# Capped attention before an eight-expert MoE on one core: the exponential of a pair of steps is issued one pair later, value products trail by seven and six steps, joint sums stand in the step without value products

## The chip, the cores and the metric

The kernel runs on one core of a Trainium2 chip. The metric is the device time of one execution in microseconds. Three runs of the kernel before took 822.85, 823.05 and 824.02 us; the median is 823.05 us. A change of 0.2%, about 1.65 us, is about what a measurement of this kernel can tell from none.

## What is computed

```python
scores = (1 / np.sqrt(64)) * np.matmul(q, k.transpose(0, 1, 3, 2))   # 8 batches, 12 heads, 448 x 448
scores = cap * np.tanh(scores / cap)                                 # cap = 30
attn = np.exp(scores - scores.max(-1, keepdims=True))
attn = attn / (attn.sum(-1, keepdims=True) + 1e-09)
x = np.matmul(attn, v)                      # laid out as 3584 tokens x 768
logits = x @ w_gate + modality_bias[modality_id]
e_idx = np.argmax(logits, axis=1)
gate_w = softmax(logits)[np.arange(N), e_idx]
for e in range(8):                          # each token goes to one expert
    h = np.maximum(x[e_idx == e] @ w1[e], 0.0)          # 768 -> 1024
    out[e_idx == e] = gate_w * (h @ w2[e])              # 1024 -> 768
```

The change lies in the attention alone; the experts follow it and are the same in both kernels.

## The kernel before

The attention is cut into 24 *units* (`ND`), each of four heads of one batch, three units to a batch. A unit has seven *steps* of 64 keys (`STEPS`), so there are 168 steps. Step `n` is step `s` of unit `d`, with `n = 7 d + s`. One loop over `n` in `attention` writes all of it out by hand; `pin` keeps an instruction in that order on its engine. Instructions without `pin` (most of the routing) are placed by the tile framework.

Work of one step:

- `scores(n)` (L489): four fp32 matmuls on quarters of the TensorE array write the 64 keys x 448 queries of four heads into a PSUM tile `sc`, of which there are two. ScalarE reads it with one tanh (L494) and writes one half of a *pair* tile `pt`; steps `2k` and `2k+1` share pair `k`. After the tanh of an odd step one exponential (L497) runs in place over the pair. Five pair tiles rotate.
- `add` (L510): VectorE adds the exponentials of a unit into `tot`, four steps behind the scores (`BEHIND`).
- `weigh(m)` (L522): four matmuls on quarters of the array multiply the exponentials of an earlier step `m` with the values and accumulate into `xT`, one PSUM tile for all units. When step 6 of a unit has been weighed, `keep` (L529) copies `xT` to SBUF on VectorE. The first value product of the next unit has to wait for that copy. How far `weigh` trails is a table: `PLAGS = (5, 5, 5, 4, 4, 4, 4)` by the step of the unit. By it, step 0 of a loop unit has two value products, step 4 has none (the *free step*), the others have one.
- `sums2` (L561, L563): in the free step of every even unit, eight matmuls on column strips make the denominators and the gate products of the last two units from their `tot` and `kept` tiles; `gl` (L567) copies the result out.
- `turn2` (L552): in step 4 of every odd unit, four transposes turn it over; VectorE takes reciprocals (L580) and products `lg` (L603).
- `start_route` and `go_on`: when a batch is complete (six times in the units 5 to 19, all odd: 5, 7, 11, 13, 17, 19), step 5 of that odd unit begins the routing: a chain of small VectorE instructions that each read the one before (`L` L250, L253, then L258 to L277, `before` and `acc` L283, L284), a small exponential on ScalarE, and two small matmuls (`rank`, L290, L292) in the next even unit.
- `tokens` (L613), a VectorE transpose, and loads and stores on SP's queue once per unit.

The last four units (`d >= PAIRED = 20`) have lags of their own (`LAGS`, `LAST`).

Of the kernel before, what the change touches and what calls it, by code (L numbers as in the profile page):

```python
# [43 lines left out]
AF = mybir.ActivationFunctionType  # L44
# [10 lines left out]
STEPS = S // KB  # L55
# [22 lines left out]
ND = NU * B  # L78
PAIRED = ND - 4
LAGS = ((5, 5, 5, 5, 4, 4, 3), (6, 5, 5, 5, 4, 4, 3))  # L80
PLAGS = (5, 5, 5, 4, 4, 4, 4)
LAST = (4, 4, 4, 4, 4, 4, 4)
BEHIND = 4

# [1 line left out]
class Program:  # L86
# [7 lines left out]
    def pin(self, inst):  # L94
        return self.tc.keep_in_program_order(inst)
# [359 lines left out]
    def attention(self, firsts, rp, xp):  # L455
        tc, nc = self.tc, self.nc
        pe, pin, V = nc.tensor, self.pin, nc.vector
        with ExitStack() as st:
# [8 lines left out]
            vas, pts, tots, kept, lgs, pays, gls, lts, raws, xss, routing = {}, {}, {}, {}, {}, {}, {}, {}, {}, {}, []  # L467

            def fetch(d):
                if d < ND:  # L470
                    for g in (2 * d, 2 * d + 1) if d else ():
                        self.load_kq(ring[g % 4], g)
                    vas[d] = ld.tile([128, VW], F32, name="va")
                    self.load(vas[d], self.v[d // NU, d % NU])

            def weights(n):
                if n % 2 == 0:
                    pts[n // 2] = pp.tile([128, 4, S], F32, name="pt")
                return pts[n // 2][:, n % 2 * 2 : n % 2 * 2 + 2]

            def scores(n):

                d, s = divmod(n, STEPS)
                sc = ps_s.tile([128, 2, 512], F32, name="sc")
                for i in range(2):
                    kq = ring[(2 * d + i) % 4]
                    for j in range(2):
                        rows = slice(j * D, (j + 1) * D)
                        pin(pe.matmul(  # L489
                            sc[i * KB : (i + 1) * KB, j, :S], kq[rows, s * KB : (s + 1) * KB], kq[rows, S:QK],  # L490
                            start=True, stop=True,
                        ))
                slow = n // STEPS == SOON + 2 and 2 <= n % STEPS <= 5
                pin(nc.scalar.activation(weights(n), sc[:, :, :S], AF.Tanh, scale=self.isc if slow else self.iscr))  # L494
                if n % 2:
                    pt = pts[n // 2]
                    pin(nc.scalar.activation(pt, pt, AF.Exp, scale=self.cabsr))  # L497

            direct = [n for d, steps in {ND - 1: 2}.items() for n in range(STEPS * d + STEPS - steps, STEPS * d + STEPS)]

# [75 lines left out]
            def turn2(a):  # L576

                lt = flip(gls.pop(a))
                for u in range(2):
                    pin(V.reciprocal(recs(a + u), lt[:, :, 2 * u : 2 * u + 2, GE : GE + 2]))  # L580
                    lts[a + u] = lt[:, :, 2 * u : 2 * u + 2]
# [12 lines left out]
            def logits(d):  # L594

                b, r = divmod(d, NU)
                lt = lts.pop(d)
                rec = pays[b][:, :, RECS:].rearrange("p c (j k) -> p c j k", j=2)
                if r == 0:
                    lgs[b] = xp.tile([CP, C, H, E], F32, name="lg", bufs=2)  # L600
                for i in range(2):
                    h0 = 4 * r + 2 * i
                    pin(V.tensor_tensor(  # L603
                        lgs[b][:, :, h0 : h0 + 2], lt[:, :, i, :GE].rearrange("p c (j e) -> p c j e", j=2),
                        rec[:, :, :, 2 * r + i].unsqueeze(3).to_broadcast([CP, C, 2, E]), op=ALU.mult,
                    ))
# [10 lines left out]
            def store(b, queue=nc.sync):  # L617
                xs = xss.pop(b).rearrange("p m k b -> p m (k b)")
                wide = KC * HB
                for g in range(4):  # L620
                    j, h = divmod(g, 2)
                    o = (2 * h + j) * wide
                    put = queue.dma_start(
                        self.xd[b * S : (b + 1) * S, o : o + wide].rearrange("(m a) f -> a m f", a=HB),
                        xs[g * HB : (g + 1) * HB],
                    )
                    if queue is nc.sync:
                        self.last_sp = pin(put).ins
# [8 lines left out]
            def go_on():  # L637
                for way in routing:
                    next(way, None)
# [13 lines left out]
            END = STEPS * ND  # L653
            due = [[] for _ in range(END + 1)]
            for m in range(END):
                d, s = divmod(m, STEPS)
                due[min(m + (LAST if d == ND - 1 else PLAGS if d < PAIRED else LAGS[d % 2])[s], END)].append(m)
            added, held = 0, range(STEPS * (SOON + 2), STEPS * (SOON + 2) + 5)

            def more(n, count=0):  # L660
                nonlocal added
                while (n not in held or count > 0) and added <= n - BEHIND + (n >= END - STEPS):
                    add(added)
                    added += 1
                    count -= 1
                    if count == 0:
                        break
# [3 lines left out]
            for n in range(END):  # L671
                d, s = divmod(n, STEPS)
                if s == 0:
                    fetch(d + 1)
                    if 1 < d < SOON and d % NU == 1:
                        store(d // NU - 1)
                    if d == 0:
                        self.fetch_bias()
                    if d == 1:
                        self.blank(xp.tile([128, FF], F32, name="spare", bufs=2))  # L680
                    if 0 <= d - 2 < CLEAR:
                        self.empty_map(d - 2)
                scores(n)
                late = False
                if not late:
                    more(n)
                if (d, s) == (1, 3):
                    self.gate_bias()
                if (s == 6 or s == 1) and d != SOON + 2:
                    go_on()  # L690
                if s == 4 and d % 2 and 3 <= d < PAIRED + 3:
                    turn2(d - 3)
                    go_on()
                    logits(d - 3)
                    logits(d - 2)
                if s == 4 and d % 2 == 0 and 2 <= d <= PAIRED:
                    sums2(d - 2)
                if (d, s) == (SOON + 1, 5):
                    sums(SOON)
                if s == 5 and d % 2 and 3 <= d < PAIRED + 2:  # L700
                    for u in (d - 3, d - 2):
                        if u % NU == NU - 1:
                            start_route(u // NU)
                if (d, s) == (SOON + 2, 2):
                    more(n, 2)
                for m in due[n]:
                    weigh(m)
                    if m % STEPS == STEPS - 1:
                        keep(m // STEPS)
                if s == 2 and d % NU == 2:  # L710
                    tokens(d - 2)
                if s == (4 if d == SOON + 1 else 6) and 0 < d < ND - 1 and d % NU != 1:
                    tokens(d - 1)
                    if d == SOON + 1:
                        store(d // NU - 1)
                if d == SOON + 2 and {2: 0, 3: 1, 4: 9}.get(s):
                    more(n, {2: 0, 3: 1, 4: 9}[s])
                if (d, s) == (SOON + 1, 6):
                    turn(SOON)
                    logits(SOON)  # L720
                    start_route(SOON // NU, firm=True)
                    go_on()
                    go_on()
                if (d, s) == (SOON + 2, 1):
                    go_on()
                    meta = self.early_slot(self.cpool, self.ps_r)
                    self.first_e = self.expert(meta, 0)
                    load_w1((0, 1), self.first_e)
                if (d, s) == (SOON + 2, 4):
                    maps = self.rows(meta, 0, early=True)  # L730
                    got = self.gather(maps, known=NT - S)
                    load_w1((2, 3, 4, 5), self.register(nc.gpsimd, meta[0:1, 0:1], E - 1, got.ins), nc.gpsimd)
                if d == SOON + 3 and s >= STEPS - TW:
                    self.norm(maps, s - (STEPS - TW))
# [20 lines left out]
            last = []  # L755
# [577 lines left out]
```

## Time and profile before

| | |
|---|---|
| median of three runs | 823.05 us (822.85 to 824.02) |
| the profiled execution | 822.63 us, of which its span is 821.0 us |
| TensorE's granted clock | 0.998 of full speed over the span |
| busy over the span | PE 803.3 us, VectorE 519.3 us, ScalarE 516.3 us, GpSimd 140.2 us |
| attention | first tanh at 7.57 us, last exponential of the attention ends at 300.5 us |

Times in the rows count from the span's start. In the timeline, equal instructions that follow each other on an engine are one row ("x8"); each fp32 matmul of the program shows as two instructions, so the four matmuls of a step are a row "x8". A busy PE is not a full PE, since the ends of matmuls are modelled; the starts of successive rows tell more.

### The profile page before, as it was taken

What the parts mean: (1) busy time and instruction counts of PE and PEld (TensorE: products, weight loads), DVE (VectorE), ACT (ScalarE), POOL (GpSimd) and SP (SyncE); (2) the same over time, 40 slices, a digit from 0 to 9 for tenths busy, and PEclk for the clock granted to TensorE, in tenths of its full rate; (3) what the DMA queues carried; (4) which work ended last, traced back from release to release, by engine and by line L of the source; (5) the groups of instructions that cost most, each with busy time, mean ns of one, the idle gap of its engine ahead of it and who ended that gap; (6) DMA issues with size and microseconds to landing.
All of it is one profiled execution on the core that took longest, in us unless ns stands there. A gap on an engine that the chain in (4) does not pass through costs nothing. (4 is left out here: it accounts for less than half of the span.)

```text
span 821.0 us, 15448 instructions
## 1 busy us (share of the span) xinstructions
PE 803.3 (98%) x5988; PEld 608.8 (74%) x5988; DVE 519.3 (63%) x865; ACT 516.3 (63%) x655; POOL 140.2 (17%) x163
## 2 busy tenths in 40 slices
PE   7999999999999999999999999999999999999996
PEld 2333333333333348999999999999999999989996
DVE  4778888888788988764445354452544635447662
ACT  6999999999999994453444334444254442556572
POOL 2000220012021230451303113031120310111010
PEclk9999999999999999999999999999999999999999
DMA  5375536255453652977656365563665545557670
GB/s 180 122 224 187 156 118 203 91 182 167 150 160 136 188 200 63 265 250 270 217 172 219 125 213 214 189 209 129 205 232 182 212 146 178 167 201 242 217 231 20
DMA packets 57011, 148.44 MB, mean 181 GB/s; under 512 B 7758, under 2 KB 22366, under 8 KB 56928
## 3 DMA queue, kind: packets, MB, share of 16 engines
q1 hardware_dynamic: 48224, 113.34, 43.1%
q0 software_dynamic: 8560, 34.02, 11.4%
q8 instruction: 49, 0.80, 0.4%
q14 instruction: 34, 0.28, 0.1%
q10 hardware_dynamic: 144, 0.00, 0.0%
HBM read 114.44 MB, written 24.64 MB: 169 GB/s over the span
## 5 line engine op out<-in xcount | busy, mean ns | idle before, releaser
L957 PE MATMUL ph<-x,al 128*128 128x384 f32 (+2 forms) x510 | 160.3, 314 | 0.0
L1010 PE MATMUL py<-bh,hh 128*128 128x384 f32 x464 | 158.8, 342 | 0.4 <-ACT hh L968 0.2
L1010 PE MATMUL py<-bl,hh 128*128 128x384 f32 x464 | 155.8, 336 | 0.0
L1010 PE MATMUL py<-bh,hl 128*128 128x384 f32 x464 | 155.7, 336 | 0.0
L522 PE MATMUL xT<-pt,va 64*64 64x448 f32 x1344 | 151.6, 538 | 0.5 <-DVE xT L529 0.5
L494 ACT ACTIVATE pt<-sc 128x896 f32<-128x896 f32 x164 | 142.8, 905 | 11.3 <-PE sc L489 11.2
L497 ACT ACTIVATE pt<-pt 128x1792 f32<-128x1792 f32 x84 | 142.7, 1698 | 2.7
L510 DVE TENSOR_TENSOR tot<-tot,pt 128x896 f32<-128x896 f32 x118 | 127.8, 1083 | 10.8 <-ACT pt L497 6.4
L953 PE MATMUL ph<-x,ah 128*128 128x384 f32 x366 | 122.6, 335 | 0.0
L954 PE MATMUL ph<-x,ah 128*128 128x384 f32 x366 | 122.4, 335 | 0.0
L896 DVE TENSOR_TENSOR bl<-raw,bh 128x768 fp32r<-128x768 f32 x88 | 81.3, 955 | 50.7 <-ACT bh L895 50.6
L522 PEld LDWEIGHTS xT<-pt,va 64*64 64x64 f32 x1344 | 50.6, 133 | 72.9 <-issue 68.4
L1026 ACT ACTIVATE ot<-py,mt 128x384 f32<-128x384 f32 (+1 forms) x58 | 33.4, 577 | 105.9 <-PE py L1010 68.6
L968 ACT ACTIVATE hh<-ph 128x384 fp32r<-128x384 f32 x64 | 31.3, 492 | 106.1 <-PE ph L957 97.9
L957 PEld LDWEIGHTS ph<-x,al 128*128 128x128 f32 x510 | 96.2, 189 | 0.0
L1010 PEld LDWEIGHTS py<-bh,hh 128*128 128x128 f32 x464 | 87.1, 188 | 1.1 <-ACT hh L968 0.5
L896 DVE TENSOR_TENSOR al<-raw,ah 128x1024 fp32r<-128x1024 f32 x60 | 70.9, 1222 | 26.7 <-ACT ah L895 26.7
L1010 PEld LDWEIGHTS py<-bl,hh 128*128 128x128 f32 x464 | 87.2, 188 | 0.0
L1010 PEld LDWEIGHTS py<-bh,hl 128*128 128x128 f32 x464 | 87.1, 188 | 0.0
L895 ACT CAST bh<-raw 128x768 fp32r<-128x768 f32 x88 | 70.0, 836 | 22.4 <-DMA raw<-in_w_dram 20.9
L489 PE MATMUL sc<-kq 64*64 64x448 f32 x672 | 79.6, 548 | 4.5 <-ACT pt L494 3.2
L923 DVE TENSOR_TENSOR x<-ptr,x 128x384 fp32r<-128x384 f32 (+2 forms) x64 | 31.6, 516 | 76.0 <-ACT x L922 76.0
(183 smaller groups left out, 957.6 us busy)
## 6 DMA issues: line engine op xcount, KB each, us to landing
raw<-in_w_dram SPq DMA_DIRECT2D x88, 384.0 KB, 4.5
raw<-in_w_dram SPq DMA_DIRECT2D x62, 512.0 KB, 4.3
kq<-in_kq_dram SPq DMA_DIRECT2D x24, 448.0 KB, 3.9
va<-in_v_dram SPq DMA_DIRECT2D x24, 448.0 KB, 5.4
kx<-in_kq_dram SPq DMA_DIRECT2D x24, 448.0 KB, 4.1
xd<-xs SPq DMA_DIRECT2D x32, 336.0 KB, 6.3
xr<-xg POOLq DMA_DIRECT2D x24, 384.0 KB, 3.1
mapd<-spare SPq DMA_DIRECT2D x4, 480.0 KB, 6.7
```

The lines of the kernel that those rows point to most:

```text
L489: pin(pe.matmul(sc[i * KB : (i + 1) * KB, j, :S], kq[rows, s * KB : (s + 1) * KB], kq[rows, S:QK], start=True, stop=True,))
L494: pin(nc.scalar.activation(weights(n), sc[:, :, :S], AF.Tanh, scale=self.isc if slow else self.iscr))
L497: pin(nc.scalar.activation(pt, pt, AF.Exp, scale=self.cabsr))
L510: pin(V.tensor_tensor(tots[d], pt_of(n - 1) if s == 1 else tots[d], pt_of(n), op=ALU.add))
L522: pin(pe.matmul(self.xT[j * D : (j + 1) * D, i, :S], vas[d][rows, o : o + D], pt[rows, j], start=s == 0, stop=s == STEPS - 1,))
L895: keep((cast.tensor_copy if cast else self.nc.scalar.copy)(hi, raw))
L896: keep((minus or self.nc.vector).tensor_tensor(lo, raw, hi, op=ALU.subtract))
L953: keep(nc.tensor.matmul(ph[:, :w], hi[:, fs], self.x[:, k, 0, :w], start=first, stop=False))
L954: keep(nc.tensor.matmul(ph[:, :w], hi[:, fs], self.x[:, k, 1, :w], start=False, stop=False))
L957: keep(nc.tensor.matmul(ph[:, :w], lo[:, fs], self.x[:, k, 0, :w], start=False, stop=last))
L1010: nc.tensor.matmul(pys[half][:, :HALF], self.h[a][:, f, rows], self.w2s[f][c][:, cs], start=f == i == 0, stop=f == FC - 1 and i == 2,)
L1026: put = nc.scalar.mul(ot[:, half * HALF :][:, :cut], pys[half][:, :cut], mt[:, t, 1:2])
```

## The change

The exponential of pair `k` follows the tanh of step `2k+3`, not that of step `2k+1`, up to step 126 (`APART`); at step 127 two exponentials stand in a row, and from there each follows its own tanh again. Value products of the units 0 to 17 trail by seven steps (step 0 to 3 of a unit) or six (4 to 6). By this table step 3 has two value products and step 6 has none. Units 18 and 19 have tables that lead back to the old lags (`CLOSER`). The joint sums move from step 4 to step 6 of an even unit, except in unit 20. `turn2` stays in step 4 and `start_route` in step 5 of an odd unit; `add` stays four steps behind.

```diff
-PLAGS = (5, 5, 5, 4, 4, 4, 4)
+PLAGS = (7, 7, 7, 7, 6, 6, 6)
+CLOSER = ((7, 7, 6, 6, 5, 5, 5), (6, 5, 5, 5, 4, 4, 4))
+APART = STEPS * (PAIRED - 2)
...
+            expd = [0]
...
                 if n % 2:
-                    pt = pts[n // 2]
-                    pin(nc.scalar.activation(pt, pt, AF.Exp, scale=self.cabsr))
+                    last = n // 2 if n > APART else n // 2 - 1
+                    while expd[0] <= last:
+                        pt = pts[expd[0]]
+                        pin(nc.scalar.activation(pt, pt, AF.Exp, scale=self.cabsr))
+                        expd[0] += 1
...
-                due[min(m + (LAST if d == ND - 1 else PLAGS if d < PAIRED else LAGS[d % 2])[s], END)].append(m)
+                lags = LAST if d == ND - 1 else LAGS[d % 2] if d >= PAIRED else CLOSER[d % 2] if d >= PAIRED - 2 else PLAGS
+                due[min(m + lags[s], END)].append(m)
...
-                if s == 4 and d % 2 == 0 and 2 <= d <= PAIRED:
+                if s == (4 if d == PAIRED else 6) and d % 2 == 0 and 2 <= d <= PAIRED:
                     sums2(d - 2)
```

In the changed kernel the lines of the attention have numbers higher by 4 to 7: tanh L498, exponential L503, `add` L517, `weigh` L529, `keep` L536, transposes L559, `L` L252.

**VectorE, an odd unit that begins a routing.** Before, from the copy of `xT` (`keep`) on (`lt` holds the transposes, `lg` the gate products, `L` to `acc` the routing):

```order
L529 COPY xT<-xT 128x896
L580 RECIPROCAL pay_778<-lt 112x4x2x2 x2
L603 TENSOR_TENSOR lg<-lt,pay_778 112x4x16 x4
L510 TENSOR_TENSOR tot<-pt 128x896
L250 TENSOR_REDUCE L<-lg 112x32
L253 TENSOR_TENSOR L<-L,bias 112x32
L510 TENSOR_TENSOR tot<-tot,pt 128x896
L258 TENSOR_REDUCE mx<-L 112x4
```

Now:

```order
L610 TENSOR_TENSOR lg<-lt,pay_767 112x4x16 x4
L252 TENSOR_REDUCE L<-lg 112x32
L255 TENSOR_TENSOR L<-L,bias 112x32
L517 TENSOR_TENSOR tot<-pt 128x896
L260 TENSOR_REDUCE mx<-L 112x4
L261 TENSOR_TENSOR L<-L,mx 112x32
L273 SCALAR_TENSOR_TENSOR sc<-L,desc 112x32
L277 TENSOR_REDUCE first<-sc 112x4
L279 TENSOR_TENSOR oh<-sc,first 112x32
L285 TENSOR_TENSOR before<-before,oh 112x8 x3
L286 TENSOR_TENSOR acc<-before,oh 112x8
L536 COPY xT<-xT 128x896
```

The copy stood ahead of the reciprocals (L587 now, just above these rows); it now stands behind them, the whole chain from `L` to `acc` and one add. It stands so in the units 5, 7, 11, 13 and 17. In the units 3, 9 and 15, which begin no routing, and in the even units, one add stands in front of it.

**TensorE, the same stretch of an odd unit**, around the scores of step 4. Before (the first row is the last product into the unit's `xT`, the last row the first into the next unit's):

```order
L522 MATMUL xT<-pt,va 64x448 x4
L489 MATMUL sc<-kx 64x448 x4
L552 MATMUL lt<-ident,gl 112x128 x4
L489 MATMUL sc<-kx 64x448 x4
L522 MATMUL xT<-pt,va 64x448 x4
```

Now (the second row of products is the last into the unit's `xT`, the third the first into the next unit's):

```order
L493 MATMUL sc<-kx 64x448 x4
L559 MATMUL lt<-ident,gl 112x128 x4
L529 MATMUL xT<-pt,va 64x448 x4
L493 MATMUL sc<-kx 64x448 x4
L529 MATMUL xT<-pt,va 64x448 x4
L493 MATMUL sc<-kx 64x448 x4
L493 MATMUL sc<-kq 64x448 x4
L529 MATMUL xT<-pt,va 64x448 x4
```

The transposes stood in the free step, behind the last product of the unit; they now stand two products ahead of it.

## Rows read from the trace of the kernel before

**Rows 1.** Engines' busy time by stretch, attention from 60 to 250 us (stretch, length, busy)
```profile
60.00:250.00 190.00, 189.18 (x1920) 71.30 (x1918) 159.43 (x284) 183.53 (x171) 22.59 (x30) 1.00 0.50 159
```
**Rows 2.** The page's groups, ScalarE's two of the attention (count, busy us, mean ns, idle)
```profile
L494 ACT ACTIVATE pt<-sc 128x896 f32<-128x896 f32 x164 | 142.8, 905 | 11.3 <-PE sc L489 11.2
L497 ACT ACTIVATE pt<-pt 128x1792 f32<-128x1792 f32 x84 | 142.7, 1698 | 2.7
```
**Rows 3.** Waits from 20 to 295 us (us in total, times, longest)
```profile
PE xT L522 <- DVE xT L529: 0.5, 1, 0.5
ACT pt L494 <- PE sc L489: 7.7, 18, 1.2
```
**Rows 4.** Timeline of ScalarE and its period (start us, length us)
```profile
98.45 1.70 ACT L497 ACTIVATE pt<-pt 128x1792 f32<-128x1792 f32 x1
...
100.06 1.70 ACT L494 ACTIVATE pt<-sc 128x896 f32<-128x896 f32 x2
...
101.79 1.70 ACT L497 ACTIVATE pt<-pt 128x1792 f32<-128x1792 f32 x1
...
105.26 1.70 ACT L497 ACTIVATE pt<-pt 128x1792 f32<-128x1792 f32 x1
...
178.36 1.70 ACT L497 ACTIVATE pt<-pt 128x1792 f32<-128x1792 f32 x1
```
**Rows 5.** Timeline of TensorE: products and scores of plain steps
```profile
117.08 0.93 PE L522 MATMUL xT<-pt,va 64*64 64x448 f32 x8
...
118.59 0.93 PE L522 MATMUL xT<-pt,va 64*64 64x448 f32 x8
```
**Rows 6.** Timeline of TensorE: around joint sums, rank and transposes
```profile
96.17 0.93 PE L489 MATMUL sc<-kx 64*64 64x448 f32 x8
...
107.82 0.97 PE L489 MATMUL sc<-kq 64*64 64x448 f32 x8
...
109.50 1.22 PE L563 MATMUL glog<-xT,wgt 128*32 128x448 f32 x8
...
110.65 0.98 PE L489 MATMUL sc<-kq 64*64 64x448 f32 x8
...
112.21 0.93 PE L489 MATMUL sc<-kq 64*64 64x448 f32 x8
...
113.28 0.98 PE L522 MATMUL xT<-pt,va 64*64 64x448 f32 x8
```
**Rows 7.** Timeline of VectorE and TensorE: unit 7 from its copy through routing
```profile
96.42 1.09 DVE L529 COPY xT<-xT 128x896 f32<-128x896 f32 x1 [1.16 <-PE xT L522]
...
97.04 0.65 PE L552 MATMUL lt<-ident,gl 128*112 128x128 f32 x4
...
97.67 0.98 PE L489 MATMUL sc<-kx 64*64 64x448 f32 x8
97.72 0.37 DVE L580 RECIPROCAL pay<-lt 112x16 f32<-112x16 f32 x2 [0.21 <-PE lt L552]
98.02 0.62 DVE L603 TENSOR_TENSOR lg<-lt,pay 112x64 f32<-112x64 f32 x4
...
98.55 1.08 DVE L510 TENSOR_TENSOR tot<-pt 128x896 f32<-128x896 f32 x1
...
99.55 0.86 DVE L250 TENSOR_REDUCE L<-lg 112x32 f32<-112x384 f32 x1
...
100.45 0.19 DVE L253 TENSOR_TENSOR L<-L,bias 112x32 f32<-112x32 f32 x1
...
101.56 0.18 DVE L258 TENSOR_REDUCE mx<-L 112x4 f32<-112x32 f32 x1
...
102.45 0.19 DVE L277 TENSOR_TENSOR oh<-sc,first 112x32 bf16<-112x32 f32 x1
...
104.68 0.36 DVE L283 TENSOR_TENSOR before<-before,oh 112x8 bf16<-112x8 bf16 x2
...
105.07 0.16 DVE L284 TENSOR_TENSOR acc<-before,oh 112x8 bf16<-112x8 bf16 x1
```

## The prediction

> **What bounds the attention now.** I read the stretches first, then the groups, the waits and at last the timeline of each engine. From 60 to 250 us TensorE shows 189.18 of 190 us, ScalarE 183.53, VectorE 159.43 [rows 1]. So either of two engines may set the pace, and which one it is decides what the change is worth, because it helps ScalarE and leaves TensorE's work as it is.
>
> ScalarE's part of a pair is two tanh and one exponential. Two tanh in a row take 1.70 us, less than twice the 0.905 of one; the next tanh starts at 100.06 though the exponential before it ends at 98.45 + 1.70 = 100.15 [rows 2, 4]. So instructions there overlap by about 0.10 us. The exponential behind its own tanh does not: 2.7 us of idle time over 84 of them, 0.03 us each [rows 2]. Its period is 101.79 - 98.45 = 3.34 us a pair [rows 4], or 23.4 us for two units (seven pairs).
>
> TensorE's part: a group of four matmuls in a plain step comes every (118.59 - 117.08) / 2 = 0.755 us, since a score group stands between these two rows [rows 5]; that is the price of a group whatever length the row shows. Two units have 14 score and 14 value groups, 28 x 0.755 = 21.1 us. The joint sums lie between two score groups 110.65 - 107.82 = 2.83 us apart, so they cost 2.83 - 0.755 = 2.08, of which about 0.25 is a wait for `keep` inside the second row (it lasts 1.22, not 0.99 or so, and begins at 109.50) [rows 6]: 1.83 of work. The transposes: 97.67 - 96.17 - 0.755 = 0.75, with 0.05 for the restart, 0.80 [rows 6, 7]. The two rank matmuls, in two of every three pairs of units: 113.28 - 112.21 - 0.755 = 0.32, with 0.05, 0.37 [rows 6]. The sum for six units, of which two begin a routing: 3 x (21.1 + 1.83 + 0.80) + 2 x 0.37 = 71.9 us. Six units take 178.36 - 105.26 = 73.1 us [rows 4]. ScalarE alone would need 21 x 3.34 = 70.1. So TensorE is issuing for 98% of the time, and what slack there is, 1.2 us in six units or 0.40 in two, is all that any relief of other engines can return. ScalarE's waits for scores, 7.7 us in all [rows 3], are the other side of this: it is ahead of TensorE.
>
> **The change part by part.**
>
> *The exponential one pair later.* 62 exponentials no longer follow their own tanh and should overlap with the tanh in front of them as the tanh behind an exponential does: 0.03 + 0.10 = 0.13 us each, 8.1 us of ScalarE. Bounds: 0 if the gap stays, 8.1 if ScalarE set the pace. I count nothing of it by itself. What it can return is TensorE's slack, below.
>
> *Start and end of the later order.* Four tanh now come before the first exponential, so ScalarE reaches step 7 one exponential, 1.7 us, earlier; TensorE at that point has two value groups fewer behind it, 1.5 us. These cancel, and both are paid back between steps 127 and 143. There two exponentials in a row, 3.2 us, and one tanh stand before the score tile comes free, against 3.0 us of score and value groups that TensorE may do meanwhile: 0 to 1.6 us, I take 1.0. The copy of a unit between the tables `CLOSER` comes behind an add or two: 0 to 1.1 us, I take 0.5. Together 1.5 us (0 to 2.7).
>
> *The free step from 4 to 6.* The sums cost the same there. In an odd unit, though, transposes and routing stay at steps 4 and 5 and now come before the last value product and its `keep`. Before, `keep` ran at 96.42, as soon as the products ended, and the chain came after it [rows 7]. TensorE then had scores, transposes and scores to do, 2.3 us, before it wanted the next `xT`. Now it has only two score groups, 1.5 us, and VectorE takes instructions in order.
>
> The chain in the units 5, 7, 11, 13, 17, counted from the end of the transposes (97.04 + 0.65 = 97.69) with the lengths of [rows 7]:
> - reciprocals and products `lg` end at 98.02 + 0.62 = 98.64: 0.95;
> - L250 0.86 and L253 0.19, each starting some 0.03 behind the one it reads: 1.12, to 2.07;
> - the add, 1.08, overlapping by 0.09 as at 98.55: 1.0, to 3.07;
> - L258 to L277, 101.56 to 102.64, overlapping likewise: 1.0, to 4.07;
> - three `before` and `acc`: two of the former and `acc` take 104.68 to 105.23, the third another 0.2: 0.78, to 4.85;
> - `keep`, 1.09, overlapping: 1.0, to 5.85; and 0.05 to TensorE's start: 5.9 us.
>
> TensorE in that time: it restarts at 97.67 with 0.05 lost, and does value, scores, value, scores, scores: 5 x 0.755 + 0.05 = 3.8 us. **It waits 2.1 us for `xT`**, five times: 10.5 us. The least I can find is 1.5 each (had it lost 0.6 elsewhere on the way), the most 3.2 (one more add in front of the chain): 7.5 to 16. Behind the waiting product stand the scores of the next steps, so ScalarE has two score tiles to work off and then stands still; nothing covers the wait. In the units 3, 9 and 15 one add, 1.08, that waits for the newest exponential stands ahead of `keep`: needed are add rest, copy and start against 1.5 us less the end of the products; 0 to 0.6, I take 0.3: 0.9 us (0 to 1.8). Even units have the sums between and are as before, 0.25 or less.
>
> *Slack that goes.* A TensorE that waits for `keep` is no longer stopped by a full score tile as well, and faster ScalarE frees it sooner. Of the 0.40 in two units I take 0.30 as gone, over eight pairs of units: -2.4 us (0 to -3.2).
>
> *Queues.* `va` has three buffers: a load at the start of unit d needs the last product of unit d - 2, now at step 5, not 3, of unit d - 1, still ahead of it. A pair tile is wanted again at step 2k by its tanh, and its last product stands ahead of the scores of step 2k - 1. `tokens` and with it SP's stores stay at step 6; GpSimd's writes follow the rank matmuls, which keep their steps. I cost these at nothing; covers are a step or more. If a load were late, it would show as a wait on a DMA.
>
> **Sum:** 10.5 + 0.9 + 1.5 - 2.4 = +10.5 us. Behind the attention the order is the same and TensorE goes on at once, so the shift stays. Against the profiled execution: 822.6 + 10.5 = 833.1. The median of the runs is 0.4 above that execution, so 833.5 us.
>
> **A rule against this.** The profile shows the matrix engine at 99.6% busy in 60 to 250 us, but its weight loads at 71.30 of 190 us, 38%, and ScalarE at 97% [rows 1]. The Trainium skill ("Perfetto Trace Analysis", section Identifying the Most-Contended Engine) says to judge TensorE's headroom by weight-load time and useful work, not by matmul busy time. By that rule TensorE has room here, ScalarE is the bound, and the sum would be the 8.1 us of saved ScalarE time, a faster kernel. I go by the starts, 0.755 us apart without a break [rows 5], which are neither of the two measures.
>
> **Rivals.**
> - *ScalarE sets the pace* and the two score tiles only hide it. For it: 97% busy; against it: 7.7 us of waits for scores and the 98% of issue. The saving of 8.1 us would come through, `keep` would be hidden: 822.6 - 8.1 = 814.5, 814.9 on the median's scale. Chance 0.04.
> - *The copy is in time.* TensorE stays the bound, but VectorE's chain is off its path: this decides when the chain of 5.9 us shrinks under 3.8, as it would if the products after the transposes came 2 us later for another reason. Then the slack alone comes back, -2.4 to -3.2, with or without 1.5 at the close: 820 to 822, I say 820.8. For it: the copy waited on in the kernel before cost TensorE only 0.5 us once [rows 3]. Chance 0.07.
> - *It all but cancels*: waits of 0.5 us instead of 2.1 and the slack gone, 2.5 + 0.9 - 2.4: about 824. Chance 0.05.
> - *The exponential still waits*, so that nothing of ScalarE's gap goes. TensorE being the bound, less slack returns, +1: 834.5. It lies in the forecast's range.
>
> **How the numbers follow.** The forecast, copies of routing units late, has 0.84. Its own bounds: the wait of 1.5 to 2.6 in place of 2.1 gives -3.0 to +2.5; the slack -0.8 to +2.4; the close -1.5 to +1.2; the quiet units -0.9 to +0.9. Taken together without all falling one way, 829 to 837. The rivals outside it hold 0.16, so the range is left at that. Slower by over 0.2%: 0.84; within: 0.05; faster: 0.11.
>
> **What would show it.** In the profile of the changed kernel: waits of TensorE's product for `xT` on VectorE's copy, about 2 us, five times, some smaller ones; the exponential starting 0.1 us before the tanh in front of it ends; ScalarE's waits for scores grown to well over 7.7 us; periods of about 26 us in pairs of units behind a routing unit, near 24.2 otherwise. I am wrong if the copies start right behind the products, or if TensorE's groups never stood 0.755 apart to begin with.

## The result, and the profile after

| | before | after |
|---|---|---|
| median of four runs | 823.21 us (822.85 to 824.02) | 835.31 us (834.53 to 835.89) |
| span of the profiled execution | 821.0 us | 834.3 us |
| TensorE's granted clock over the span | 0.998 | 0.994 |

The ratio is 1.0145, with an interval of 1.0133 to 1.0158: 12 us slower, inside the range of 829 to 837 and 1.8 us above the forecast of 833.5. After the change the exponential is L503, the tanh L498, `add` L517, the product L529, `keep` L536.

**ScalarE got what the change offers.** The page's groups of the kernel after (count, busy us, mean ns, idle before and what ended it) answer to [rows 2]:

```profile
L498 ACT ACTIVATE pt<-sc 128x896 f32<-128x896 f32 x164 | 146.4, 916 | 30.5 <-PE sc L493 30.4
L517 DVE TENSOR_TENSOR tot<-tot,pt 128x896 f32<-128x896 f32 x118 | 127.9, 1083 | 28.2 <-ACT pt L503 25.9
L503 ACT ACTIVATE pt<-pt 128x1792 f32<-128x1792 f32 x84 | 142.4, 1697 | 0.6
```

The idle time ahead of the 84 exponentials fell from 2.7 to 0.6 us. But the tanh now wait 30.4 us for scores instead of 11.2, and VectorE's adds wait 25.9 us for the exponential in this group alone. The waits of the attention, from 20 to 315 us (us in total, times, longest), answer to [rows 3]:

```profile
DVE tot L517 <- ACT pt L503: 33.0, 35, 2.3
ACT pt L498 <- PE sc L493: 26.8, 45, 2.6
...
PE xT L529 <- DVE xT L536: 11.7, 11, 2.0
```

Before, the adds waited 3.0 us:

```profile
DVE tot L510 <- ACT pt L497: 3.0, 3, 1.1
```

The last of the three rows is the one on the path: TensorE's product waits for VectorE's copy for 11.7 us in 11 places, where before it was 0.5 us once. Unit 7, the one of [rows 7], in the timeline of all engines (start us, length us, idle before and releaser):

```profile
97.45 0.65 PE L559 MATMUL lt<-ident,gl 128*112 128x128 f32 x4
97.58 0.92 ACT L498 ACTIVATE pt<-sc 128x896 f32<-128x896 f32 x1 [0.25 <-PE sc L493]
98.40 1.69 ACT L503 ACTIVATE pt<-pt 128x1792 f32<-128x1792 f32 x1
98.43 0.62 DVE L610 TENSOR_TENSOR lg<-lt,pay 112x64 f32<-112x64 f32 x4
99.08 0.87 DVE L252 TENSOR_REDUCE L<-lg 112x32 f32<-112x384 f32 x1
100.12 1.09 DVE L517 TENSOR_TENSOR tot<-pt 128x896 f32<-128x896 f32 x1
101.13 0.18 DVE L260 TENSOR_REDUCE mx<-L 112x4 f32<-112x32 f32 x1
102.24 0.55 DVE L285 TENSOR_TENSOR before<-before,oh 112x8 bf16<-112x8 bf16 x3
102.83 0.16 DVE L286 TENSOR_TENSOR acc<-before,oh 112x8 bf16<-112x8 bf16 x1
102.91 1.08 DVE L536 COPY xT<-xT 128x896 f32<-128x896 f32 x1
104.05 1.77 PE L529 MATMUL xT<-pt,va 64*64 64x448 f32 x8 [2.03 <-DVE xT L536]
107.38 0.92 ACT L498 ACTIVATE pt<-sc 128x896 f32<-128x896 f32 x1 [2.59 <-PE sc L493]
```

From the end of the transposes, 98.10, to the product, 104.05, are 5.95 us; the forecast's chain is 5.9. TensorE stands still for 2.03 of them, and behind the late product ScalarE waits 2.59 us for its scores. The exponential starts at 98.40, 0.10 before the tanh in front of it ends (97.58 + 0.92).

The same product in the other four units and in the quiet unit 9, on TensorE's timeline:

```profile
77.99 0.98 PE L529 MATMUL xT<-pt,va 64*64 64x448 f32 x8 [1.86 <-DVE xT L536]
129.98 0.98 PE L529 MATMUL xT<-pt,va 64*64 64x448 f32 x8 [0.25 <-DVE xT L536]
155.89 0.98 PE L529 MATMUL xT<-pt,va 64*64 64x448 f32 x8 [1.89 <-DVE xT L536]
181.96 1.24 PE L529 MATMUL xT<-pt,va 64*64 64x448 f32 x8 [2.04 <-DVE xT L536]
233.84 0.98 PE L529 MATMUL xT<-pt,va 64*64 64x448 f32 x8 [1.89 <-DVE xT L536]
```

So the five waits are there, 1.86 to 2.04 us of idle time each (9.7 in all). Counted from start to start, with the 0.755 us that the group before it needs taken off, they cost 2.04, 2.21, 2.07, 2.22 and 2.07: 10.6 us. The quiet units cost 0.43 each in that way.

**What the forecast did not have** is in the stretches behind two of these waits (stretch, length, busy of PE, PEld, DVE, ACT, POOL, then the granted clock, DMA share and GB/s):

```profile
101.50:104.05 2.55, 0.52 (x9) 0.01 (x1) 2.31 (x10) 2.55 (x4) 0.26 (x2) 1.00 0.65 180
104.05:107.10 3.05, 3.05 (x18) 1.05 (x22) 2.95 (x4) 0.74 (x1) 0.00 (x0) 0.50 0.76 301
181.90:185.95 4.05, 4.00 (x25) 1.44 (x29) 3.47 (x6) 1.99 (x3) 0.00 (x0) 0.58 0.58 225
155.90:159.00 3.10, 3.10 (x36) 1.32 (x40) 3.10 (x5) 2.18 (x4) 0.00 (x0) 1.00 0.77 294
```

The clock is 1.00 up to and through the wait of unit 7 and 0.50, the lower of the two levels (1.2 GHz), for 3.05 us behind it; so it is for most of 181.90 to 185.95 behind that of unit 13. Behind that of unit 11 it stays at 1.00. What it costs, in the starts of TensorE's groups behind the waiting product, to the second product after it, unit 7 first (from 104.05), then unit 11 (from 155.89):

```profile
105.59 1.72 PE L493 MATMUL sc<-kq 64*64 64x448 f32 x8
...
108.78 0.92 PE L529 MATMUL xT<-pt,va 64*64 64x448 f32 x8
...
156.70 0.93 PE L493 MATMUL sc<-kq 64*64 64x448 f32 x8
...
158.95 0.93 PE L529 MATMUL xT<-pt,va 64*64 64x448 f32 x8
```

The scores come 1.54 us behind the waiting product in unit 7 and 0.81 in unit 11, the second product 4.73 and 3.06: 1.67 us lost. Unit 13 lost 1.69. Together 3.4 us.

**Where the time lies.** The spans differ by 13.3 us, and 12.8 of them arise between the first tanh and that of step 154. By the starts of the tanh of steps 0, 28, 126 and 154, which for the kernel after are

```profile
7.46 1.73 ACT L498 ACTIVATE pt<-sc 128x896 f32<-128x896 f32 x2 [4.59 <-PE sc L493]
53.60 1.72 ACT L498 ACTIVATE pt<-sc 128x896 f32<-128x896 f32 x2
233.81 0.91 ACT L498 ACTIVATE pt<-sc 128x896 f32<-128x896 f32 x1
287.02 0.92 ACT L498 ACTIVATE pt<-sc 128x896 f32<-128x896 f32 x1
```

and before 7.57, 54.98, 225.29 and 274.38:

| us | units 0 to 3 | units 4 to 17 | units 18 to 21 |
|---|---|---|---|
| before | 47.41 | 170.31 | 49.09 |
| after | 46.14 | 180.21 | 53.21 |
| after less before | -1.27 | +9.90 | +4.12 |

The product that waits for unit 17's copy stands behind the scores of step 126, so the fifth wait delays what follows and falls into the third column; that of unit 3 falls into the middle in the same way. The middle one holds four waits, 8.5, three quiet units, 1.3, and the low clock, 3.4, which make 13.2; that it is 9.9 leaves 3.3 us of slack returned, a remainder and not a measurement of its own.

### The profile page after: what moved, and what is told of

The parts are those of the page before. It is cut to its first block, busy times and chain, and to the rows that moved or that the text cites. A ratio compares the mean times of both kernels' runs of the same rounds, so it can differ in the third digit from the quotient of the medians.

```text
span 834.3 us, 15458 instructions
## 1 busy us (share of the span) xinstructions
PE 806.0 (97%) x5988; PEld 609.8 (73%) x5988; DVE 520.0 (62%) x865; ACT 511.9 (61%) x655; POOL 139.9 (17%) x163
## 3 DMA queue, kind: packets, MB, share of 16 engines
q0 software_dynamic: 8560, 34.02, 11.2%
## 5 line engine op out<-in xcount | busy, mean ns | idle before, releaser
L529 PE MATMUL xT<-pt,va 64*64 64x448 f32 x1344 | 153.8, 545 | 11.7 <-DVE xT L536 11.7
L498 ACT ACTIVATE pt<-sc 128x896 f32<-128x896 f32 x164 | 146.4, 916 | 30.5 <-PE sc L493 30.4
L517 DVE TENSOR_TENSOR tot<-tot,pt 128x896 f32<-128x896 f32 x118 | 127.9, 1083 | 28.2 <-ACT pt L503 25.9
L503 ACT ACTIVATE pt<-pt 128x1792 f32<-128x1792 f32 x84 | 142.4, 1697 | 0.6
L529 PEld LDWEIGHTS xT<-pt,va 64*64 64x64 f32 x1344 | 49.6, 134 | 88.3 <-issue 66.9
L312 POOL DMA_INDIRECT mapd<-pay,pos x32 | 35.6, 1112 | 268.8 <-DVE pos L305 137.0
```

The source lines that it names most:

```text
L312: put = nc.gpsimd.indirect_dma_start(self.mapd, bass.IndirectOffsetOnAxis(ap=pos[:, c : c + 1], axis=0), pay[:, c, :], None, bounds_check= ...
L517: pin(V.tensor_tensor(tots[d], pt_of(n - 1) if s == 1 else tots[d], pt_of(n), op=ALU.add))
L529: pin(pe.matmul(self.xT[j * D : (j + 1) * D, i, :S], vas[d][rows, o : o + D], pt[rows, j], start=s == 0, stop=s == STEPS - 1,))
```

## The experiments

Theory A is the prediction's: TensorE issues without a break, and the copy behind the routing chain stops it. Rival B: the later exponentials and products cost by themselves, through adds that wait for the newest exponential. Rival C is the prediction's first: ScalarE sets the pace and its 8.1 us should show when the exponential is moved back. Run 4 asks something else, whether the low clock is a consequence of TensorE's standing still. Each ratio is against the kernel before in the same comparison. Lines have moved by a few numbers in each kernel.

**1. The copy ahead of the routing.** `start_route` of units 5 to 17 is issued behind the last product and copy of its step, not ahead of it, and the chain's first instruction on VectorE (`L`) is pinned there; that edit is not shown.

```diff
-if s == 5 and d % 2 and 3 <= d < PAIRED + 2:
+if s == 5 and d % 2 and 3 <= d < PAIRED + 2 and d >= PAIRED - 1:
...
+if s == 5 and d % 2 and 3 <= d < PAIRED - 1:
+    for u in (d - 3, d - 2):
+        if u % NU == NU - 1:
+            start_route(u // NU)
```

> The changed kernel with the start of a routing (units 5 to 17) written behind that step's value product, so that the copy of xT stands ahead of the routing chain on VectorE. Theory A (TensorE waits for a late copy): the five waits of 2.0 to 2.2 us shrink to the 0.4 us of a unit without routing, and with them the two stretches at half clock (about 3 us): 835.3 - 8.5 - 3 = about 824 us. If ScalarE, which in its fixed order now meets the routing's small exponential before VectorE has its input ready, stands still instead, up to 1 us of each comes back: 824 to 829. Rival B (the later exponentials and products cost by themselves, through adds that wait for the newest exponential): 832 us or more.

Measured: 831.47 us (830.87 to 831.83), ratio 1.0095, 1.0077 to 1.0114. A miss for A's 824 to 829, and next to B's 832: the five waits are gone, the time is not. The waits of its attention, in TensorE's view and in that of all engines:

```profile
PE sc L494 <- ACT pt L499: 6.5, 10, 0.9
PE xT L530 <- DVE xT L537: 3.3, 11, 0.5
...
ACT ex L272 <- DVE L L262: 3.5, 5, 0.7
```

The longest wait for the copy is now 0.5 us. In its place ScalarE stands 0.7 us, five times, at the routing's small exponential (`ex`), which waits for VectorE's chain, late by one copy; the tanh behind it is late, no score tile is free, and TensorE waits for that, 6.5 us where it was 1.7. One wait was traded for another, as run 2 shows.

**2. The same, and the small exponential later.** It is issued one call of `go_on` later, when VectorE is done.

```diff
-if not late:
+if not late and b == 5:
     self.pin(nc.scalar.activation(ex, L, AF.Exp))
...
+if b != 5:
+    self.pin(nc.scalar.activation(ex, L, AF.Exp))
```

> As copy_first, and the routing's small exponential stands one call of the routing later on ScalarE, so that it cannot stop there. Theory A: 824 us, up to 5 us under copy_first if ScalarE's stop was real there; TensorE's waits for the copy about 0.4 us each, granted clock 1.0 throughout. Rival B: 832 us or more.

Measured: 827.16 us (826.05 to 828.75), ratio 1.0042, 1.0027 to 1.0057; clock 0.998. Against the change as it is, 0.0103 of 823 us or 8.5 us have come back, and TensorE's wait for a score tile is 2.1 us again. That is 3 us over A's 824 and 5 under B's 832: the order on VectorE makes most of the loss, not all. Units 4 to 17 take 171.07 us, 9.1 less than in the kernel after; units 18 to 21 take 52.32. The waits for the copy are not gone altogether:

```profile
PE xT L532 <- DVE xT L539: 3.3, 11, 0.5
```

Every odd unit now waits as the quiet ones do, 0.43 us from start to start. Seven of them make 3.0 us in the units 4 to 17, and the stretch is only 0.8 longer than before the change: 2.2 us of slack are returned here as well. What is left of the loss lies at the close.

**3. The exponential behind its own tanh again,** all else as in the change.

```diff
-last = n // 2 if n > APART else n // 2 - 1
+last = n // 2
```

> The changed kernel with each exponential behind its own tanh again; later products and the moved sums stay. Theory A (TensorE sets the pace): within 1.5 us of the changed kernel, 834 to 837 us, though ScalarE does 8.1 us more. Rival C (ScalarE sets the pace and the later exponential is what saves): about 843 us. Rival B, if the later exponentials delay the adds: 828 us or less.

Measured: 838.98 us (837.55 to 840.06), ratio 1.0184, 1.0161 to 1.0207: 3.2 us over the change as it is, above A's values and below C's. The gap is back:

```profile
L503 ACT ACTIVATE pt<-pt 128x1792 f32<-128x1792 f32 x84 | 142.7, 1699 | 2.8
```

Part of the 3.2 us is a third stretch at the low clock, behind the first, second and fourth of its five waits:

```profile
80.30:83.50 3.20, 3.20 (x20) 1.14 (x24) 3.17 (x4) 1.35 (x4) 0.00 (x0) 0.59 0.71 278
108.00:111.00 3.00, 2.96 (x20) 1.05 (x23) 2.86 (x3) 0.97 (x3) 0.00 (x0) 0.54 0.78 295
160.30:163.30 3.00, 3.00 (x32) 1.24 (x36) 2.97 (x4) 2.08 (x4) 0.00 (x0) 1.00 0.73 293
```

At 1.7 us for one such stretch, some 1.5 us are left as the worth of the later exponential, against 8.1 by C. By the stretches of the first table, run 3 is 1.9 us longer than the change in the units 0 to 3, 2.6 longer in the units 4 to 17, the low clock with them, and 1.1 shorter in the units 18 to 21.

**4. TensorE kept busy through the wait.** Twelve bf16 matmuls on constants, each of which fills 128x384 of a tile, stand ahead of each of the five waiting products; nothing reads what they write.

```diff
+if s == 0 and d in (6, 8, 12, 14, 18):
+    idle = ps_g.tile([128, 512], F32, name="glog", tag="glog")
+    for _ in range(12):
+        pin(pe.matmul(idle[:, :W], self.ones[:, :128], self.ones, start=True, stop=True))
```

> The changed kernel with twelve idle bf16 matmuls of 128x384 into a free PSUM tile ahead of each of the five products that wait for a late copy; about 1.9 us of work on TensorE in each wait, nothing of the result changes. If the half clock behind two of the waits comes from TensorE standing still: no stretch under 1.0, about 3 us less, 832 us. If the half clock has another cause: 835 us as before, with the two stretches.

Measured: 832.77 us (832.43 to 833.36), ratio 1.0111, 1.0092 to 1.013. The product still starts no earlier than the copy allows, but behind it the clock stays at 1.00:

```profile
104.00:108.00 4.00, 4.00 (x39) 1.67 (x40) 3.90 (x5) 2.94 (x5) 0.00 (x0) 1.00 0.82 313
180.00:184.00 4.00, 4.00 (x37) 1.71 (x38) 3.86 (x7) 2.94 (x5) 0.00 (x0) 1.00 0.85 332
```

0.0034 of 823 us, 2.8 us, come back, near the 3.4 of the timeline; the units 4 to 17 take 177.06 us, 3.1 less. So the clock fell because TensorE stood still. What is left of the loss, 0.0111 of 823 us or 9.1, is the change without the low clock; the forecast's sum, which had no such term, is 10.5.

The next three ran on another chip, on which the kernel before itself takes 832.18 us (830.68 to 834.07 in 23 runs); they are compared with that alone. The change itself was not run there; runs 8 to 11 bring the best of the three back to the first chip.

**5. Transposes and routing in the free step.** `turn2` and `start_route` go to step 6 of the odd units 3 to 17, where the copy is already done; the small exponential is late as in 2.

```diff
-if s == 4 and d % 2 and 3 <= d < PAIRED + 3:
+if s == (6 if d < PAIRED - 1 else 4) and d % 2 and 3 <= d < PAIRED + 3:
...
-if s == 5 and d % 2 and 3 <= d < PAIRED + 2:
+if s == (6 if d < PAIRED - 1 else 5) and d % 2 and 3 <= d < PAIRED + 2:
```

> The changed kernel with the transposes and the start of a routing moved on into the new free step 6 of an odd unit (units 3 to 17), so that they again follow the copy of xT, and the routing's small exponential one call later. Theory A (the copy's place costs): TensorE's long waits go, no half clock: about 827 us, like copy_first_late_exp, and the rest over the kernel before lies in the adds and in the two pairs of units where the old order is resumed. Rival B (later exponentials and products cost by themselves): 832 us or more.

Measured: 831.5 us (830.2 to 832.93), ratio 0.9991, 0.9982 to 1.0, on A's side and, on another chip, under run 2's 1.0042. No loss against the kernel before is left, and nothing is won.

**6. The same, with the adds six steps behind** up to the end of unit 18.

```diff
-while (n not in held or count > 0) and added <= n - BEHIND + (n >= END - STEPS):
+while (n not in held or count > 0) and added <= n - (6 if n < STEPS * 19 else BEHIND) + (n >= END - STEPS):
```

> As turn_free, and the adds trail the scores by six steps, not four, up to step 132, so that no add stands on VectorE waiting for the newest exponential in front of a copy. If adds that wait for the later exponential are what is left (0.43 us at each odd unit, and the joint sums behind them): about 4 us less than turn_free, 822 to 823.5 us, level with the kernel before. If they cost nothing: as turn_free.

Measured: 827.15 us (826.67 to 830.27), ratio 0.9947, 0.9934 to 0.9961. The adds' wait for the exponential, in run 5 and then here:

```profile
DVE tot L519 <- ACT pt L505: 33.1, 31, 2.7
```
```profile
DVE tot L519 <- ACT pt L505: 1.7, 3, 1.0
```

The change moved the exponential one pair later and left the adds four steps behind, so that 31 of them in run 5 met an exponential that was not done; that wait was worth 0.0044 of 832 us, 3.7 us. TensorE's listed waits for copies and score tiles differ by only 0.1 us (6.7 and 6.8) between the two, because the list has no wait inside a row. The joint sums have one: their second half reads a copy, too. In run 5 and then here, behind the same unit:

```profile
87.76 1.85 PE L572 MATMUL glog<-xT,wgt 128*32 128x448 f32 x8
```
```profile
86.00 0.94 PE L572 MATMUL glog<-xT,wgt 128*32 128x448 f32 x8
```

Added up from start to start over the units 4 to 17, the joint sums take 2.7 us less here and the products that wait for a copy 2.2 less; 0.8 is lost in other places, and the stretch is 4.1 us shorter (170.03 against 174.16).

**7. The same as 6, with the exponential behind its own tanh** (the edit of 3).

> As turn_free_add6, with each exponential behind its own tanh: what the later exponential itself is worth once no copy is late. Theory A (TensorE sets the pace, the slack is some 0.4 us in two units): 1 to 3 us above turn_free_add6. Rival C (ScalarE sets the pace): 8 us above.

Measured: 830.58 us (829.29 to 832.49), ratio 0.9981, 0.9972 to 0.9991. In a kernel without the five waits the later exponential is worth 0.0034 of 832 us, 2.8 us, a third of the 8.1 us that ScalarE saves. By stretch it is 2.4 in the units 0 to 3 and 2.4 in the units 4 to 17, while behind them the later exponential costs 2.0. The second figure is near the slack that TensorE has to give (2.4 of a possible 3.2 in the forecast) and far from the 6.4 that the 49 exponentials of that stretch save at 0.13 each: there C falls. In the units 0 to 3 it doesn't, as the first point of the next section shows.

**8 to 11. Repeats on the chip of runs 1 to 4,** on which the kernel before takes 823.26 us: the kernel before itself, the change, the kernel of run 2 and that of run 6.

> The kernel before, profiled beside the others on one chip, since its time is 823 us on one chip and 832 us on another. Same as its own runs; the profile shows which of its stretches are longer there, if this chip is of the slower kind.

> The changed kernel on the same chip: ratio to the kernel before 1.013 to 1.016 where that takes 823 us. If the extra time of a slower chip lies in stretches that TensorE's late copies cover anyway, the ratio is smaller there, 1.005 to 1.012.

> copy_first_late_exp on the same chip. Theory A: five late copies and the half clock are gone, ratio to the kernel before 1.003 to 1.006 where that takes 823 us; what is left sits in the pairs of units 18 to 21.

> turn_free_add6 on the same chip: by the periods of its trace (23.7 us in quiet pairs of units against 24.1 before, 2 to 3 us lost again in units 18 to 21) level with the kernel before or up to 0.5% faster: ratio 0.994 to 1.001.

| | us | ratio | interval |
|---|---|---|---|
| before, again | 823.69 | 1.0001 | 0.9988 to 1.0015 |
| after, again | 836.09 | 1.0154 | 1.0134 to 1.0173 |
| run 2 again | 826.28 | 1.0032 | 1.0021 to 1.0044 |
| run 6 again | 821.77 | 0.9981 | 0.9969 to 0.9992 |

The change repeats, with the low clock behind the same two waits. Run 6 beats both kernels: 1.6 us under the one before, 14 under the change. Its waits for the copy and for the exponential:

```profile
PE xT L531 <- DVE xT L538: 1.5, 2, 1.0
```
```profile
DVE tot L519 <- ACT pt L505: 1.2, 2, 1.0
```

By the stretches of the first table it takes 45.17, 167.60 and 52.85 us: 2.2 and 2.7 won, 3.8 lost in the units 18 to 21, where the order goes back to the old lags. TensorE's value products of that stretch, before and then here (eight rows to a product group, their number behind the x):

```profile
225.29:274.38 49.09, 23.70 (x212) 8.07 (x216) 1.00 0.45 139
```
```profile
221.49:274.34 52.85, 26.03 (x236) 8.63 (x236) 1.00 0.47 134
```

Three groups more, 2.3 us at 0.755 each, are work left over from the units 0 to 3, which have 176 rows instead of 200. The rest lies mainly in starts behind a copy or a full score tile, about 1 us each.

The profiled execution of run 6 here was the slowest of its twelve, 824.27 us, and yet its attention is shorter. What varies from one execution to the next lies behind the attention: from the start of its last exponential to the end the kernel before took 522.2 us in its first profile and 523.7 in run 8, while the three stretches of the two agree within 0.05 us.

## Why the prediction was right, and where its sum was off

- **TensorE is the bound, not ScalarE.** Right from unit 4 on. The later exponential took the gap that it was to take (idle 2.7 to 0.6 us), and moved the time by some 1.5 us in run 3 and 2.8 in run 7, not by 8.1; the starts 0.755 us apart were the sign that held. The Trainium skill ("Perfetto Trace Analysis", section Identifying the Most-Contended Engine) has TensorE's headroom judged by weight-load time and useful work; taken by weight loads alone, 38%, as room on TensorE, that is not borne out here. In the units 0 to 3, which the forecast's stretch from 60 us on left out, ScalarE is the busier one in the kernel before (busy of PE, PEld, DVE, ACT):

```profile
7.57:54.98 47.41, 43.82 (x448) 15.93 (x444) 33.16 (x44) 46.63 (x42) 2.26 (x7) 1.00 0.54 164
```

  It waits 0.3 us there behind its first tanh, and moving the exponential back costs 1.9 us in run 3 and 2.4 in run 7.
- **Five waits of 2.1 us for the late copy, 10.5.** Right in place, number and size: 10.6. The chain added up from single rows was 5.9 us and is 5.95 in unit 7. Runs 1 and 2 show that the order on VectorE causes it.
- **The quiet units, 0.9.** 1.3 from start to start: 0.25 of idle time each, and the restart, which this term left out.
- **Start and close, 1.5.** The order's begin gave 1.3 us back, where it was taken to cancel; the close lost 4.1, of which 2.1 are the fifth wait. Net +0.8. The forecast priced both ends by both engines; in the trace ScalarE sets the pace at the begin, where fewer value products save nothing, and TensorE at the close, where they are made up. In run 2, without that wait, it is -1.3 + 3.2 = +1.9, so the term was about right, but its two halves were not.
- **Slack, -2.4.** -3.3 as a remainder. It comes back without the long waits, too: 2.2 us in run 2, and 2.7 in the units 4 to 17 of run 6 on the first chip, where no product waits for a copy. Run 7 gives 2.4 of it up with the exponential moved back. So the size was right, and of the forecast's two reasons the faster ScalarE is enough; the other, that a TensorE which waits for `keep` isn't stopped by a full score tile as well, is not shown.
- **What failed in the sum** is a term that isn't there: the wait was taken to cost its own length. Behind two of five, TensorE ran at half its clock for some 3 us, 1.7 us lost each, 3.4 in all. The sum with what was measured: 10.6 + 1.3 + 0.8 + 3.4 - 3.3 = 12.8 us, by which the way from the first tanh to that of step 154 is longer; it closes because the slack is the remainder. That the forecast came within 1.8 us is in part luck: of the missing 3.4, 0.9 of slack and 0.7 at the ends made up about half. Six units, of which the remainder is no part, show the same. From the exponential at 111.37 to that at 189.27,

```profile
111.37 1.71 ACT L503 ACTIVATE pt<-pt 128x1792 f32<-128x1792 f32 x1
...
189.27 1.69 ACT L503 ACTIVATE pt<-pt 128x1792 f32<-128x1792 f32 x1
```

  they take 77.9 us, against 73.1 in [rows 4]. With the one low-clock stretch in it, 1.7, taken off it is 76.2; TensorE's work by the forecast with its waits, and no slack, is 71.9 + 2 x 2.1 + 0.3 = 76.4.
- **A price named too small:** that the add waits for the newest exponential was seen for three quiet units alone. It happens 35 times, and run 6 puts it at 3.7 us in a kernel without the five waits. That is what rival B had right.

## What to carry to other kernels

When work is moved across an in-order queue, list what now stands between a buffer's last writer and the copy that frees it, and add up the chain's rows against what the waiting engine still has to do: here that gave 2.1 us where 2.0 to 2.2 were measured. An engine that issues all the time gives back only its slack when another is relieved (2.2 to 3.3 us of 170 here), so look stretch by stretch which engine that is; and a producer that is moved later wants its consumers on the next engine moved by as much (adds six steps behind instead of four: 3.7 us). A stall of TensorE may be followed by a stretch at half clock, so price it with a part on top, and look at the granted clock of the stretch behind it.

## What the hardware did that was not expected

- A stall of 2 us in a TensorE that had been issuing without a break was followed by about 3 us at 0.50 of full clock, two times in five after the change and three in five in run 3; with matmuls on constants in the stall it did not happen. The length of the idle time alone doesn't decide: after the change the two of 2.03 and 2.04 us were followed by it and the three of 1.86 to 1.89 were not, but in run 3 those of 1.92, 1.93 and 1.93 were and those of 1.94 and 1.95 were not:

```profile
108.04 1.67 PE L529 MATMUL xT<-pt,va 64*64 64x448 f32 x8 [1.92 <-DVE xT L536]
...
160.27 0.98 PE L529 MATMUL xT<-pt,va 64*64 64x448 f32 x8 [1.94 <-DVE xT L536]
```

  What decides stays open.
- The kernel before takes 823 us on the chip of runs 1 to 4 and 8 to 11 and 832 on that of runs 5 to 7, 1% apart, with medians that repeat. A difference of a few us between kernels could only be read from runs on one chip. The kernel of run 6 has a trace from each: the units 0 to 3 take 45.2 us on both and the part from the last exponential on 523.9 on the first and 522.2 on the second, but from step 28 to that exponential it is 244.9 and 250.5, at a granted clock of 1.00 on both. So the second chip's extra time lies in the attention from unit 4 on; why stays open.
